# One pattern pass of the VectorE exponential moved to an accumulating GpSimd DMA

## The chip, the cores and the metric

One Trainium2 chip, one core of it. The metric is the device time of one execution, in microseconds (us), lower is better. The kernel before takes 898.37 us (median of 3 runs, 897.88 to 899.86). Experiments ran in groups on one chip each, together with new runs of the kernel before. A run counts as slow when it is over 1.5% above the fastest run of the same kernel; all are fast unless it is told otherwise.

## The reference

Two attention layers side by side, each with 2048 rows, width 512 and 32 heads of 16. A is attention within four causal segments, with a memory of the earlier segments mixed in; B is plain attention over all 2048 keys. B holds most of the exponentials, and they are what this case is about.

```python
def _B_ref(x, wqkv, wo):
    B, S, D = x.shape                     # 1, 2048, 512
    H = 32
    Dh = D // H                           # 16
    qkv = (x @ wqkv).reshape(B, S, 3, H, Dh).transpose(2, 0, 3, 1, 4)
    q, k, v = qkv[0], qkv[1], qkv[2]
    p = softmax(einsum('bhqd,bhkd->bhqk', q, k) * Dh ** -0.5)
    o = einsum('bhqk,bhkd->bhqd', p, v)
    return o.transpose(0, 2, 1, 3).reshape(B, S, D) @ wo
# _A_ref: per segment of 512 rows a causal softmax (mask) and p @ v, then
#   o = g * (phi(q) @ M) / (phi(q) @ z) + (1 - g) * a_dot;  M += phi(k)^T v;  z += sum phi(k)
# the result: concatenate([A, B], axis=-1), bf16
```

## The kernel before

The kernel is software-pipelined by its own planner. While it is built, it keeps a clock for each engine (`T["pe"]`, `T["dve"]`, `T["pool"]`, `T["sp"]` for SyncE's queue) and decides at each step what TensorE does next. What comes out is **one fixed order of instructions for each engine**; semaphores then make each wait for its inputs. If something is later on the chip than the plan assumed, TensorE does not pick other work. It waits.

Exponentials are computed in two places. ScalarE does tiles of two or three PSUM banks (`pT`). VectorE takes over whole blocks of four banks by a bit trick: it scales a score so that, as an integer, it is the bit pattern of an fp16 number near the exponential, and takes four such patterns with four offsets (`LADDER`). The products of all four with V are added in PSUM, so that their errors average out.

```python
LADDER = (12914, 13046, 13325, 13628)
VBUFS = 10                                # shared tiles of 128 x 2048 x 2 bytes
...
def v_pick():                             # start a block?
    ...
    if vlive[0] > VBUFS - 2:
        return False
    ...
            vlive[0] += 1
            x = wk.tile([P, 4, 512], U16, name="vx", tag="vx", bufs=VBUFS)
            vnow[0] = (u, kb, x, list(q4))

def v_evac(u, kb, x, j, vt, end):         # four a block: bank j of scores -> first pattern
    def f():
        pin(nc.vector.tensor_scalar(x[:, j, :], vt[:], XSCALE, float(LADDER[0]), ALU.mult, ALU.add))
        if end:
            buf = [len(LADDER)]
            v_ready(u, kb, x, buf)
            for off in LADDER[1:]:        # three pattern passes
                later(0.70, v_rung(u, kb, x, off, buf), ...)

def v_rung(u, kb, x, off, buf, pool=False):
    def f():
        vlive[0] += 1
        p = wk.tile([P, 4, 512], U16, name="vx", tag="vx", bufs=VBUFS)
        ...
        pin(nc.vector.tensor_scalar(p[:], x[:], float(off - LADDER[0]), 32767.0, ALU.add, ALU.min))
        v_ready(u, kb, p, [1], ...)
        v_done(buf)

def v_ready(u, kb, p, buf, at=None):      # from this planned time on, TensorE may read the tile
    pd = p[:].bitcast(F16)
    pvq.append(dict(u=u, kb=kb, v=buf, ready=(T["dve"] + DVEEND if at is None else at) + 0.06, ...))
```

`pin` keeps an instruction in program order against its neighbours on the engine. Two other users of SyncE's queue matter below: the eight small transfers that spread a query tile, and the transposes (four for an input chunk, four for the keys of the memory).

```python
for e in range(2):                        # do_q: eight transfers of 16 KB
    for j in range(4):
        r = slice(32 * j + DH * e, 32 * j + DH * e + DH)
        nc.sync.dma_start(out=dst[r, e, :], in_=qc[r, :])
        on_sp(0.5, T["dve"] + 0.1)
...
for cc in range(4):                       # load_xT
    nc.sync.dma_start_transpose(t[:, cc, :], xs[name][ch * W:(ch + 1) * W, cc * P:(cc + 1) * P])
```

`zero()` multiplies by zeros where TensorE would otherwise have little to do; it is meant to keep the clock up. By the planner's own count it aims at an activity of 0.52 over about 3 us, in which a product on a quarter of the array counts 0.25; that this is the right aim is not tested here.

## Time and profile before

| | before |
|---|---|
| time, median | 898.37 us |
| ScalarE busy | 866.6 of 897.7 us |
| ScalarE exponential tiles / VectorE blocks | 747 / 125 |
| VectorE busy | 796.1 us |
| TensorE waits for VectorE, all kinds | 6.7 us |
| DMA traffic | 19.85 MB, 22 GB/s |
| TensorE at half clock | 19 us |

The last row is summed from the trace's clock records (some 2 us of it, in every kernel, lie after the last instruction), and it is the one that I undervalued. From the page of the kernel before: the clock in 40 slices of 22 us, and the group of TensorE products that read VectorE's patterns (busy us, mean ns, idle us before them, what ended most of it).

```profile
PEclk9999999979999999999999999999999999999998
...
L117 PE MATMUL acc<-vx,VB 128*32 128x512 f16 x2000 | 180.8, 384 | 2.0 <-DVE vx L982 0.7
```

The clock is down in one slice only, beside the end. Stage by stage around it (us from the start; PE, PEld, DVE, ACT and POOL busy with counts; clock; DMA share; GB/s):

```profile
150.00:186.00 36.00, 30.54 (x268) 10.03 (x266) 29.60 (x55) 33.61 (x32) 11.39 (x23) 0.98 0.20 41
186.00:196.00 10.00, 9.52 (x49) 1.89 (x48) 4.90 (x9) 5.47 (x5) 2.31 (x2) 0.56 0.07 13
```

TensorE's single stop of 5 us ends at 186.5; the ten microseconds from 186 on run at a mean clock of 0.56. TensorE is busy there (9.52 of 10) and the engines that it feeds are not: ScalarE is busy for 5.47 us of 10. **The wait is paid a second time, afterwards.**

### The profile page before, as it was taken

Reading aid. Unit: us, or ns where it says so; the run is one execution under the profiler, and the core shown is the slowest. Engines: PE = TensorE matmul, PEld = TensorE weight load, DVE = VectorE, ACT = ScalarE, POOL = GpSimd, SP = SyncE. Lnnn points to the kernel's source line nnn. Section 1 sums busy time; section 2 is a strip of 40 time slices with the busy share of each in tenths; the row PEclk is TensorE's granted clock in tenths of the full one; section 3 lists DMA queues with packets and bytes.
Section 4 is the critical chain, followed back from the end, with each engine's and each line's share of the span. In section 5 each row is a group of like instructions: output and inputs, shape, how many; then the busy total and the mean of one; then the engine's idle time right before and its main releaser. Section 6 shows DMA issues by size and latency. Waiting matters only on the chain.

```text
span 897.7 us, 19235 instructions
## 1 busy us (share of the span) xinstructions
PE 863.9 (96%) x7673; PEld 258.9 (29%) x7673; DVE 796.1 (89%) x1362; ACT 866.6 (97%) x777; POOL 130.8 (15%) x295
## 2 busy tenths in 40 slices
PE   9999999979999999999999999999999999999996
PEld 3322332312323232222232322323222322222222
DVE  4786699959998998989989999999999999999994
ACT  6999999969999999999999999999999999999995
POOL 7710300310202003030110302002030300000000
PEclk9999999979999999999999999999999999999998
DMA  9600000200001201000000210000000000000000
GB/s 194 140 10 12 24 18 9 48 18 7 15 6 19 60 23 28 7 7 13 2 19 2 42 37 12 3 1 7 1 8 1 19 24 13 1 2 1 1 2 29
DMA packets 48181, 19.85 MB, mean 22 GB/s; under 512 B 37200, under 2 KB 48080, under 8 KB 48080
## 3 DMA queue, kind: packets, MB, share of 16 engines
q1 hardware_dynamic: 46736, 17.99, 9.1%
q8 instruction: 62, 1.02, 0.5%
q10 hardware_dynamic: 1344, 0.52, 0.2%
q14 instruction: 39, 0.32, 0.1%
HBM read 4.20 MB, written 4.19 MB: 9 GB/s over the span
## 4 chain that ended last, share of the span: by engine, by line
ACT 25%; PE 21%; issue 9%; DVE 5%; POOL 0%; DVEq 0%; ACTq 0%
ACT pT L893 24%; PE acc L117 11%; PE s_ps L117 6%; PE v_ps L117 2%; DVE vx L966 2%; DVE vx L982 2%; PE o_ps L117 1%; DVE tT L382 1%; ACT ex L307 0%; POOL pT L903 0%; PE l_ps L117 0%; PE q_ps L117 0%; DVE OT_b L430 0%; DVE rsum L405 0%; DVE osb L1264 0%
## 5 line engine op out<-in xcount | busy, mean ns | idle before, releaser
L893 ACT ACTIVATE pT<-s_ps 128x1536 bf16<-128x1536 f32 x747 | 854.9, 1289 | 13.0 <-PE s_ps L117 8.8
L966 DVE TENSOR_SCALAR vx<-v_ps 128x512 uint16<-128x512 f32 x500 | 328.4, 685 | 26.8 <-PE v_ps L117 21.6
L117 PE MATMUL s_ps<-qb,KB 32*128 32x512 bf16 x1548 | 249.4, 384 | 8.2 <-ACT pT L893 4.0
L982 DVE TENSOR_SCALAR vx<-vx 128x2048 uint16<-128x2048 uint16 x375 | 248.9, 693 | 5.0 <-PE v_ps L117 3.2
L117 PE MATMUL v_ps<-qb,KB 32*128 32x512 bf16 x500 | 181.8, 382 | 2.0 <-DVE vx L966 0.9
L117 PE MATMUL acc<-vx,VB 128*32 128x512 f16 x2000 | 180.8, 384 | 2.0 <-DVE vx L982 0.7
L903 POOL TENSOR_SCALAR_AFFINE_SELECT pT<-pT 128x256 bf16<-128x256 bf16 (+2 forms) x241 | 105.8, 469 | 481.8 <-ACT pT L893 481.3
L117 PE MATMUL acc<-pT,VB 128*32 128x512 bf16 x1548 | 151.6, 389 | 0.0
L117 PEld LDWEIGHTS <-KB 32*128 32x128 bf16 x2048 | 82.8, 91 | 237.1 <-issue 230.2
L117 PE MATMUL acc<-zeros 128*128 128x512 bf16 x395 | 135.4, 389 | 0.0
L117 PEld LDWEIGHTS <-VB 128*32 128x32 bf16 x3548 | 73.4, 94 | 165.6 <-issue 154.1
L117 PE MATMUL s_ps<-qa,kA 32*128 32x384 bf16 (+3 forms) x512 | 53.3, 299 | 5.3 <-ACT pT L893 3.0
L117 PEld LDWEIGHTS <-zeros 128*128 128x128 bf16 x417 | 34.2, 98 | 82.5 <-issue 77.2
L382 DVE STREAM_TRANSPOSE tT<-acc 128x512 f32<-128x512 f32 x64 | 44.9, 704 | 12.8 <-PE acc L117 12.4
L117 PE MATMUL acc<-pT,vA 128*32 128x256 bf16 (+3 forms) x512 | 33.3, 306 | 0.3 <-POOL pT L903 0.2
L117 PEld LDWEIGHTS <-kA 32*128 32x128 bf16 x512 | 17.8, 91 | 45.3 <-issue 42.3
L272 DVE CAST qc<-q_ps 128x512 bf16<-128x512 f32 x28 | 19.1, 684 | 6.8 <-PE q_ps L117 6.6
L117 PE MATMUL q_ps<-xT_a,w_a 128*128 128x512 bf16 x64 | 19.8, 386 | 5.0 <-DMA xT_a<-in_A_x_dram 5.0
L460 DVE CAST osb<-o_ps 128x512 bf16<-128x512 f32 x28 | 19.1, 683 | 4.6 <-PE o_ps L117 4.1
L416 POOL TENSOR_TENSOR tN<-tT,rsum 128x512 bf16<-128x512 f32 x1 | 1.4, 1368 | 130.1 <-DVE rsum L405 130.1
L117 PE MATMUL k_ps<-xT_a,w_a 128*128 128x512 bf16 x64 | 19.8, 398 | 0.0
L117 PE MATMUL o_ps<-wo_a,OT_a 128*128 128x512 bf16 x64 | 18.8, 383 | 0.3 <-DVE vx L966 0.2
(94 smaller groups left out, 409.7 us busy)
## 6 DMA issues: line engine op xcount, KB each, us to landing
out_dram<-osb SPq DMA_DIRECT2D x30, 128.0 KB, 1.7
w_b<-in_B_wqkv_dram SPq DMA_DIRECT2D x3, 512.0 KB, 6.0
qb<-qc SPq DMA_DIRECT2D x96, 16.0 KB, 1.8
qa<-qc SPq DMA_DIRECT2D x72, 16.0 KB, 1.8
phk<-phkT SPq DMA_TRANSPOSE x48, 2.4
w_a<-in_A_wv_dram SPq DMA_DIRECT2D x1, 512.0 KB, 5.1
wo_a<-in_A_wo_dram SPq DMA_DIRECT2D x1, 512.0 KB, 5.0
wo_b<-in_B_wo_dram SPq DMA_DIRECT2D x1, 512.0 KB, 4.9
```

Source lines behind the costliest of these rows:

```text
L117: return pin(nc.tensor.matmul(out, lhsT, rhs, **k))
L272: pin(nc.vector.tensor_copy(qc[:], ps[:]))
L382: pin(nc.vector.transpose(st["tT"][:, e].rearrange("p c d -> p (c d)"), acc[:]))
L416: pin(eng.tensor_tensor(o, tT[:, :, :, 0:DH], rr.to_broadcast(bc), op=ALU.mult))
L460: pin(nc.vector.tensor_copy(osb[:], ps[:]))
L893: pin(nc.scalar.activation(pT[:, 0:n, :], pt[:, 0:n, :], ACT.Exp, scale=SCALE))
L903: pin(nc.gpsimd.affine_select(out=blk, in_=blk, compare_op=ALU.is_ge, fill=0.0, base=0, pattern=[[0, len(sls)], [1, P]], channel_multiplie ...
L966: pin(nc.vector.tensor_scalar(x[:, j, :], vt[:], XSCALE, float(LADDER[0]), ALU.mult, ALU.add))
L982: pin(nc.vector.tensor_scalar(p[:], x[:], float(off - LADDER[0]), 32767.0, ALU.add, ALU.min))
```

## The change

The intent is to relieve VectorE of one of its three passes a block, so that it can take over more blocks from ScalarE, the bound. A tile is filled with the constant difference of the offsets by a plain DMA on SyncE's queue when the block starts. After the block's last evacuation, a DMA issued from GpSimd adds the first pattern to it (`accum_op`). Two more of the shared tiles are made, the output weights move into shared tiles, and all transfers on SyncE are pinned.

```diff
-VBUFS = 10
+VBUFS = 12
+DMARUNG = 3
+ACCPOOL = 1.05
+ACCDMA = 4.5
+FILLSP = 0.55
+FILL = 512
 ...
+        fill = wk.tile([P, 1, FILL], I16, name="fill")
+        nc.gpsimd.memset(fill[:], LADDER[DMARUNG] - LADDER[0])
 ...  v_pick
-            if vlive[0] > VBUFS - 2:
+            if vlive[0] > VBUFS - 3:
 ...
-                vnow[0] = (u, kb, x, list(q4))
+                vlive[0] += 1
+                p = wk.tile([P, 4, 512], I16, name="vx", tag="vx", bufs=VBUFS)
+                pin(nc.sync.dma_start(out=p[:].rearrange("p j (a c) -> p (j a) c", c=fill.shape[-1]),
+                                      in_=fill[:].to_broadcast([P, 2048 // fill.shape[-1], fill.shape[-1]])))
+                on_sp(FILLSP, T["pe"])
+                vnow[0] = (u, kb, (x, p), list(q4))
 ...  v_evac
-                    for off in LADDER[1:]:
-                        later(0.70, v_rung(u, kb, x, off, buf), ...)
+                    for i in range(1, len(LADDER)):
+                        if i == DMARUNG:
+                            atasks.append((T["dve"] + DVEEND, v_sum(u, kb, *x, buf)))
+                            continue
+                        later(0.70, v_rung(u, kb, x[0], LADDER[i], buf), ...)
 ...
+        def v_sum(u, kb, x, p, buf):
+            def f():
+                pin(nc.gpsimd.dma_start(out=p[:], in_=x[:], accum_op=ALU.add))
+                v_ready(u, kb, p, [1], T["pool"] + ACCDMA)
+                v_done(buf)
+            return f
 ...  pool_run
+            while atasks and (atasks[0][0] < T["pe"] + 0.1 or not live[0]):
+                ready, f = atasks.popleft()
+                on_pool(ACCPOOL, ready)
+                f()
 ...  (cut: pin() around every transfer on SyncE; output weights into shared tiles; a removed GpSimd path)
```

Note what the plan knows and does not know. It lets TensorE read the sum 1.05 + 4.5 us after the accumulation is planned to start. It lets the accumulation start when the pattern is ready, and never asks whether the fill has landed.

> **What bounds the kernel now.** I read the page's busy shares first, then the groups of ScalarE and VectorE, then the busy time stage by stage, then the one stage that stands out.
>
> The busy shares, columns: engine, busy microseconds, share of the span, instructions; below them two costly groups (busy, mean ns of one, idle before them and what ended it).
>
> ```profile
> PE 863.9 (96%) x7673; PEld 258.9 (29%) x7673; DVE 796.1 (89%) x1362; ACT 866.6 (97%) x777; POOL 130.8 (15%) x295
> ...
> L893 ACT ACTIVATE pT<-s_ps 128x1536 bf16<-128x1536 f32 x747 | 854.9, 1289 | 13.0 <-PE s_ps L117 8.8
> L966 DVE TENSOR_SCALAR vx<-v_ps 128x512 uint16<-128x512 f32 x500 | 328.4, 685 | 26.8 <-PE v_ps L117 21.6
> ...
> L982 DVE TENSOR_SCALAR vx<-vx 128x2048 uint16<-128x2048 uint16 x375 | 248.9, 693 | 5.0 <-PE v_ps L117 3.2
> ...
> L117 PE MATMUL acc<-zeros 128*128 128x512 bf16 x395 | 135.4, 389 | 0.0
> ```
>
> ScalarE does 747 exponential tiles and waits only 13.0 us ahead of them: it sets the pace. TensorE looks as full (96%), but 135.4 us of it are multiplications by zeros that only fill gaps. VectorE computes the exponentials of 125 blocks by itself: four evacuations (500 in all) and three pattern passes (375) a block. It is at 89%, with no room for many more blocks. So work leaves ScalarE only if VectorE is relieved first; that is the intent.
>
> The same by stages (us from the start; PE, PEld, DVE, ACT, POOL busy with counts; granted clock; DMA share; GB/s):
>
> ```profile
> 0.00:22.00 22.00, 20.04 (x123) 6.97 (x123) 9.08 (x18) 13.06 (x14) 16.12 (x45) 1.00 0.95 198
> 22.00:100.00 78.00, 76.55 (x626) 23.15 (x626) 58.09 (x99) 77.62 (x71) 21.70 (x53) 1.00 0.23 51
> 100.00:250.00 150.00, 141.81 (x1206) 43.08 (x1202) 128.05 (x232) 141.50 (x131) 26.77 (x55) 0.97 0.09 19
> 250.00:400.00 150.00, 146.51 (x1319) 43.56 (x1317) 138.07 (x234) 148.99 (x135) 21.16 (x47) 1.00 0.09 22
> 400.00:550.00 150.00, 146.95 (x1346) 44.06 (x1339) 141.50 (x248) 149.61 (x136) 15.37 (x33) 1.00 0.08 18
> ...
> 860.00:897.70 37.70, 29.08 (x251) 8.92 (x248) 24.90 (x46) 27.01 (x25) 0.78 (x2) 0.91 0.06 18
> ```
>
> ScalarE's 31 idle us lie at the start (22 - 13.06 = 8.9), at the end (10.7) and in one middle stage (150 - 141.5 = 8.5, granted clock 0.97); elsewhere it misses under 1 us per 150. The timeline of that middle stage shows why:
>
> ```profile
> 178.68 4.96 SPq L277 DMA_DIRECT2D qa<-qc  x8
> ...
> 183.68 1.26 SPq L234 DMA_TRANSPOSE xT_a<-in_A_x_dram  x1
> 186.48 0.59 PE L117 MATMUL q_ps<-xT_a,w_a 128*128 128x512 bf16 x1 [5.04 <-DMA xT_a<-in_A_x_dram]
> ...
> 188.63 1.45 ACT L893 ACTIVATE pT<-s_ps 128x1536 bf16<-128x1536 f32 x1 [5.02 <-PE s_ps L117]
> ```
>
> The fourth transpose of an input chunk stands in SyncE's queue behind eight small transfers of a query tile (4.96 us). TensorE, which runs its instructions in a fixed order, stands still for 5.04 us, and every engine with it.
>
> **What the Trainium skill says.** "DMA: Bandwidth & Descriptors", section "SWDGE vs HWDGE vs iDMA": accumulation during a DMA is possible only for one issued from GpSimd, which writes the descriptors in software. No accumulating transfer is in this trace, so it shows nothing of its cost. The same page, "Anatomy of one DMA", fits a transfer as 2.0 us + bytes/436 GB/s; for 512 KB that is 3.2 us (estimate from that page). Here the 512 KB weight loads from HBM land 4.9 to 6.0 us after issue, so it is optimistic for those. "SBUF — State Buffer", section "Who interferes with whom": a VectorE instruction in a two-port mode and GpSimd lock each other out, and descriptor writing suffers. The trace fits: GpSimd's 128x128 mask of 0.352 us mean took 0.80 us where it began together with a pattern pass, at 444.60 us:
>
> ```profile
> 444.60 0.65 DVE L982 TENSOR_SCALAR vx<-vx 128x2048 uint16<-128x2048 uint16 x1
> 444.60 0.80 POOL L903 TENSOR_SCALAR_AFFINE_SELECT pT<-pT 128x128 bf16<-128x128 bf16 x1 [44.84 <-ACT pT L893]
> ```
>
> **The change, part by part.** Counts come from the order of the built instructions, durations from the rows above.
>
> ScalarE: VectorE blocks go from 125 to 132, so ScalarE loses 7 blocks of four banks: 1868 banks become 1840. A bank costs 854.9/1868 = 0.458 us, so 28 banks are 12.8 us. This is on the path.
>
> VectorE: evacuations 500 to 528, +28 x 0.657 (328.4/500) = +18.4 us; pattern passes 375 to 264, -111 x 0.664 = -73.7 us. Busy falls from 796 to about 741 us. Worth nothing directly; the seven blocks are what it buys. The plan takes so few although VectorE is freed: a block now holds two of the 12 tiles from its first score on, and none may start above nine live.
>
> TensorE: 112 more products with the pattern tiles (+10.1 us at 180.8/2000), 28 more single scores (+10.2), 28 fewer tile scores and products (-7.2), 23 fewer zero products (-7.9): +5 us, inside what zeros fill today.
>
> DMA: 132 fills and 132 accumulations of 512 KB, 138 MB beside today's 19.85 MB: some 156 GB/s on average over 885 us. It fits the engines, but each accumulation also reads its destination; if that doubles the moved part of the fit, it needs 2.0 + 2 x 1.2 = 4.4 us (estimate). The diff plans with 1.05 us on GpSimd and 4.5 us to land.
>
> GpSimd: 132 issues at about 1.05 us, +139 us, to about 270 of 885: not a bound, but in order with the causal masks.
>
> SyncE's queue: the diff pins every transfer to program order. In the new order the four transposes of the chunk of 174.8 us stand together, and the query tile follows. The hole at 183 us should go: -8.5 us, on the path. I count this as surely as the ScalarE term.
>
> What is given back. TensorE's order is fixed, so a late pattern tile stops it. By ScalarE's pace (0.458 us a bank) I counted, in the built order, from the last score of a block to the first reader of its accumulated tile: median 7.8 us, tenth percentile 6.9, shortest 3.2. Score and evacuation take 0.38 + 0.69 us plus signalling, some 1.4; 5.5 are left at the tenth percentile, against 1.05 + 4.4 = 5.5. It just fits. The chain that starts at the fill is tighter: 3.2 + 1.05 + 4.4 = 8.7 us, against a median of 10.5 from the fill's place in SyncE's queue to the reader. About 14 fills stand over 2 us behind query tiles (4.93 us for eight transfers) and transposes (some 5 us for four). Nine blocks have under 8.7 us: 1.9, 5.5, 5.5, 5.9, 6.0, 7.4, 7.7, 7.8, 8.5; shortfalls sum to 22 us. ScalarE has about one tile, 1 us, in hand each time, which leaves 13; a few will overlap other slack. I take +9 us.
>
> Sum: 898.4 - 12.8 - 8.5 + 9 = 886 us.
>
> **Rivals.** First, the accumulation is slower than planned, or GpSimd's descriptors are held up by the two remaining passes, which start just when the accumulation is issued (both follow the last evacuation). 107 of the 132 tiles are read as the last of their block, some at the planned moment; 1 us more than the slack on a hundred blocks gives about +80 us after what ScalarE has in hand: 960. For it: the 0.80 us mask above, and no measurement of this kind of transfer. Against it: the diff's constants look like measured ones, and leave that slack. Second, everything lands in time: 898.4 - 21.3 = 877 us, 2.4% faster. For it: ScalarE's other waits are tiny. Against it: the nine blocks. Third, transfers of fills and accumulations lengthen each other and the query tiles (now 1.8 us to landing), a few us per chunk: 895 to 905. Fourth, VectorE's relief is worth more than the seven blocks: hardly, as ScalarE waits so little elsewhere.
>
> **Range and chances.** The sure terms sum to -21 us, and 2% is 18 us; 3.4 us of new waits suffice to fall under it. I give 0.23 to faster, 0.57 to within 2%, and 0.20 to slower, nearly all of it the first rival. Range 870 to 915.
>
> **What would show it.** ScalarE's tiles at 736 and busy near 854 us; VectorE near 741; no 5 us wait for the A input near 180 us and a clock of 1.00 there; waits of TensorE's products for an accumulating DMA, in a handful of places of 2 to 6 us, behind SyncE's query tiles; issue to landing of the accumulations near 4 to 5.5 us, of the fills near 3 to 4. Wrong: waits for that DMA at most blocks (first rival), or almost none (second); ScalarE's idle time in the middle over 20 us without any DMA behind it would mean that I have missed a mechanism.

## The result, and the profile after

The changed kernel took 972.3 us (median of 4 runs, 966.53 to 975.56), the kernel before 899.09 us on the same occasion (897.88 to 899.86). The ratio is 1.0809 (95% interval 1.075 to 1.0867): 8% slower, and outside the predicted range. Ratios here are the mean time of one kernel's fast runs over that of the other's of the same rounds, so not quite the ratio of the medians quoted.

From the page after: busy shares; groups; clock; issues with their median time to landing.

```profile
PE 885.0 (91%) x7730; PEld 257.3 (27%) x7730; DVE 754.4 (78%) x1280; ACT 860.9 (89%) x766; POOL 245.3 (25%) x431
...
PEclk9999998989969989799798997999999999899999
...
L910 ACT ACTIVATE pT<-s_ps 128x1536 bf16<-128x1536 f32 x736 | 848.7, 1274 | 88.6 <-PE v_ps L121 48.5
L988 DVE TENSOR_SCALAR vx<-v_ps 128x512 uint16<-128x512 f32 x528 | 348.9, 686 | 114.0 <-PE v_ps L121 106.3
L1002 POOL DMA_DIRECT2D vx<-vx x132 | 121.9, 924 | 606.4 <-DVE vx L988 476.1
...
L121 PE MATMUL acc<-vx,VB 128*32 128x512 f16 x2112 | 199.5, 402 | 53.7 <-DMA vx<-vx 52.0
...
L1011 DVE TENSOR_SCALAR vx<-vx 128x2048 uint16<-128x2048 uint16 x264 | 179.8, 690 | 3.6 <-DMA vx<-vx 2.0
...
vx<-fill SPq DMA_DIRECT2D x132, 512.0 KB, 4.7
vx<-vx POOLq DMA_DIRECT2D x132, 512.0 KB, 5.2
```

The work moved as planned: ScalarE has 736 tiles, VectorE 264 passes. No engine is the bound by its work any more. ScalarE's wait ahead of its tiles rose from 13.0 to 88.6 us, and the clock is down in ten slices (two before). The products that read VectorE's patterns, which had waited 2.0 us, wait 53.7, of which 52.0 for the accumulating transfer. Its median of 5.2 us to landing is about what the plan has (1.05 + 4.5 = 5.55); asked for all 132, the trace gives a minimum of 4.5, a median of 5.2 and a maximum of 8.1 us. The fills give 3.2, 4.7 and 8.5.

The view of waits after (us in total, times, longest):

```profile
PE acc L121 <- DMA vx<-vx: 52.0, 31, 10.5
ACT pT L910 <- PE v_ps L121: 48.5, 44, 10.3
...
POOL vx L1002 <- DMA vx<-fill: 40.7, 5, 17.8
```

Only 31 waits, not one for each of 132 blocks, and the longest is 10.5 us. The timeline shows how that one came about. First SyncE's queue (start, us, engine, line, what, times):

```profile
254.18 5.61 SPq L281 DMA_DIRECT2D qa<-qc  x8
260.21 4.96 SPq L342 DMA_TRANSPOSE phk<-phkT  x4
265.29 3.97 SPq L959 DMA_DIRECT2D vx<-fill  x4
```

then GpSimd, TensorE and ScalarE (in brackets the idle time before, and what ended it):

```profile
271.13 0.86 POOL L1002 DMA_DIRECT2D vx<-vx  x1 [17.76 <-DMA vx<-fill]
...
277.27 0.62 PE L121 MATMUL acc<-vx,VB 128*32 128x512 f16 x4 [10.48 <-DMA vx<-vx]
...
278.53 1.02 ACT L910 ACTIVATE pT<-s_ps 128x1024 bf16<-128x1024 f32 x1 [10.26 <-PE v_ps L121]
```

Four fills stand behind eight query transfers and four transposes in one queue. The fill lands just before 271.13, the accumulation needs 6.1 us more, and the products that the fixed order put there stop TensorE, and with it everything, for 10.5 us. Its stages:

```profile
250.00:268.00 18.00, 16.19 (x142) 4.76 (x135) 16.03 (x28) 18.00 (x18) 0.88 (x1) 1.00 0.35 84
268.00:286.00 18.00, 8.73 (x56) 1.83 (x55) 4.57 (x7) 4.77 (x5) 2.58 (x3) 0.53 0.81 203
286.00:300.00 14.00, 13.48 (x137) 4.16 (x135) 12.69 (x23) 13.69 (x13) 2.91 (x3) 1.00 0.83 208
```

The clock fell to half at 268.7 us and stayed there for 17.1 us, well past the end of the wait: ScalarE was busy for 4.77 of 18 us. In the stage after, the clock is full and ScalarE is busy for 13.69 of 14 us, with as much traffic (208 GB/s), so traffic of that size does not by itself stop it.

**The half clock.** The Trainium skill, "TensorE: Matmul & The Clock Gate", section "Part 1: The HAM clock gate (the "warmup" mystery)", says that TensorE's clock is full or half, decided by how busy it was in windows of about 3.4 us, and its section "HAM oscillation — how this bites in real kernels" tells of a kernel that waits for DMA and starts each tile at half clock. The traces agree: the records know only 1.0 and 0.5, and the half periods away from the ends, in these two traces, last 3.4, 6.8, 10.2, 13.7 or 17.1 us. They sum to 111 us after and 19 us before. I could have read this before predicting, from the stage of 0.56 above, and did not.

A much shorter stop can be enough. This one is from the same kernel, a wait of 0.93 us that began at 321.2 us and had nothing to do with an accumulation:

```profile
322.15 0.37 PE L121 MATMUL v_ps<-qb,KB 32*128 32x512 bf16 x1 [0.93 <-DVE osb L466]
```

and the stages before and after 323.3 us:

```profile
319.50:323.30 3.80, 2.87 (x27) 0.74 (x26) 2.91 (x6) 3.12 (x4) 0.00 (x0) 1.00 0.78 235
323.30:326.70 3.40, 3.40 (x13) 0.68 (x13) 2.31 (x4) 2.73 (x4) 0.84 (x1) 0.50 0.70 237
```

Over all seventeen traces of this case (before, after and the fifteen experiments; TensorE's stops that began at full clock, from 25 us on), this is how often a half period began by 3.5 us after the stop:

| length of the stop, us | stops | followed by half clock |
|---|---|---|
| 0.8 to 1 | 39 | 7 |
| 1 to 1.5 | 44 | 12 |
| 1.5 to 2 | 31 | 24 |
| 2 to 3 | 41 | 35 |
| over 3 | 45 | 45 |

So a wait is not worth its length alone: in these traces a stop of over 2 us was followed by a half period in 80 of 86 cases, one of 0.5 to 0.8 us in 16 of 97. (Some short stops have other stops close by. Of those with none over 0.5 us within 3.5 us, 3 of 29 of 0.8 to 1 us and 11 of 40 of 1 to 1.5 us were followed by one.)

**Where the 71 us went.** The spans differ by 968.7 - 897.7 = 71.0 us. ScalarE's busy time fell by 5.7 (866.6 to 860.9), so its idle time rose by 76.7. Directly, TensorE's waits for accumulations are 52. The half clock grew by 92 us; the rest, about 25 us, is 0.27 of that. The 0.27 is an estimate fitted to this one trace, not a measured cost; the experiments below test it.

**Behind the 52 us.** Followed block by block (130 of the 132 could be matched), 45 accumulated tiles were read within 0.3 us of landing, so TensorE stood ready for them, or nearly. For 21 blocks the fill landed after the last evacuation. 14 of the 45 stand behind such late fills, and TensorE's waits for these sum to 37 of the 52 us; all those fills came after query tiles or transposes in SyncE's queue. The other 15 us stand behind fills that were in time; there the accumulation took longer than the plan had room for (of all 132, 53 needed more than the planned 5.55 us, and about a tenth over 6.8).

### The profile page after: what moved, and what is told of

Same layout as the page of the kernel before. It is cut to its first block, busy times and chain, and to the rows that moved or that the text cites. A ratio compares the mean times of both kernels' runs of the same rounds, so it can differ in the third digit from the quotient of the medians.

```text
span 968.7 us, 19889 instructions
## 1 busy us (share of the span) xinstructions
PE 885.0 (91%) x7730; PEld 257.3 (27%) x7730; DVE 754.4 (78%) x1280; ACT 860.9 (89%) x766; POOL 245.3 (25%) x431
## 3 DMA queue, kind: packets, MB, share of 16 engines
q1 hardware_dynamic: 116176, 87.07, 29.6%
## 4 chain that ended last, share of the span: by engine, by line
PE 32%; DMA 22%; issue 21%; ACT 13%; DVE 8%; POOL 2%; SPq 1%; POOLq 0%; DVEq 0%; ACTq 0%
DMA vx<-vx 15%; PE acc L121 14%; ACT pT L910 12%; PE s_ps L121 9%; DMA vx<-fill 5%; PE v_ps L121 5%; DVE vx L988 3%; POOL vx L1002 2%; PE o_ps L121 2%; DVE vx L1011 2%; PE k_ps L121 1%; PE q_ps L121 1%; ACT ex L311 1%; SPq L238 1%; DVE tT L386 1%
## 5 line engine op out<-in xcount | busy, mean ns | idle before, releaser
L910 ACT ACTIVATE pT<-s_ps 128x1536 bf16<-128x1536 f32 x736 | 848.7, 1274 | 88.6 <-PE v_ps L121 48.5
L988 DVE TENSOR_SCALAR vx<-v_ps 128x512 uint16<-128x512 f32 x528 | 348.9, 686 | 114.0 <-PE v_ps L121 106.3
L1002 POOL DMA_DIRECT2D vx<-vx x132 | 121.9, 924 | 606.4 <-DVE vx L988 476.1
L121 PE MATMUL s_ps<-qb,KB 32*128 32x512 bf16 x1520 | 259.2, 400 | 8.5 <-ACT pT L910 6.0
L121 PE MATMUL acc<-vx,VB 128*32 128x512 f16 x2112 | 199.5, 402 | 53.7 <-DMA vx<-vx 52.0
L121 PE MATMUL v_ps<-qb,KB 32*128 32x512 bf16 x528 | 196.7, 402 | 3.5 <-DVE vx L988 1.5
L1011 DVE TENSOR_SCALAR vx<-vx 128x2048 uint16<-128x2048 uint16 x264 | 179.8, 690 | 3.6 <-DMA vx<-vx 2.0
L121 PE MATMUL acc<-pT,VB 128*32 128x512 bf16 x1520 | 155.4, 405 | 0.0
L121 PEld LDWEIGHTS <-VB 128*32 128x32 bf16 x3632 | 79.3, 95 | 232.3 <-issue 219.6
L121 PE MATMUL k_ps<-xT_b,w_b 128*128 128x512 bf16 x64 | 20.0, 399 | 0.2 <-DVE tT L386 0.2
```

The lines of the kernel that those rows point to most:

```text
L121: return pin(nc.tensor.matmul(out, lhsT, rhs, **k))
L910: pin(nc.scalar.activation(pT[:, 0:n, :], pt[:, 0:n, :], ACT.Exp, scale=SCALE))
L988: pin(nc.vector.tensor_scalar(x[0][:, j, :], vt[:], XSCALE, float(LADDER[0]), ALU.mult, ALU.add))
L1002: pin(nc.gpsimd.dma_start(out=p[:], in_=x[:], accum_op=ALU.add))
```

## The experiments

The first explanation was: *the pattern tiles come late against the fixed order, because the plan leaves too little time for accumulation, or fill, or both.* Rivals: SyncE's queue alone; the traffic itself (163 GB/s) slows everything; the rest of the change (pins, twelve buffers, output weights) does it; GpSimd's descriptor writing is locked out by VectorE. The expectations name theories as they stood at that time; where one missed, it is said below.

Fifteen kernels ran, in four groups on different occasions; all were correct. Medians of the kernel before in the groups: 897.69 (first four kernels below: pins, fill by GpSimd DMA, memset, fill in the plan), 897.27 (7.0, 3.0, all late, no DMA pass), 898.18 (6.0, 8.5, 7.0 with hold, 7.0 with fill and query), 897.91 (the last three). Two other builds did not run. One, meant to add the traffic without the dependence, did not fit into SBUF, so **traffic alone was never tried**. The other (7.0 with the fill landing in the plan) was REFUSED by the check: an accumulation was left unissued at the end of the plan, and an uninitialised read followed; it was mended as the run "7.0 with fill and query".

### Pins alone

```diff
 kernel before
-            nc.sync.dma_start_transpose(t[:, cc, :], ...)
+            pin(nc.sync.dma_start_transpose(t[:, cc, :], ...))
 ... the same on every other SyncE transfer
```

> The kernel before, with nothing changed but that every SyncE transfer is pinned to program order; the order on TensorE is identical, 125 blocks and 747 ScalarE tiles. If the 5.04 us wait for the A input (and the 10.2 us of half clock after it) is priced as I priced it in the prediction, -8.5 us: about 890 us. Rival: the pin moves a transfer that delays something else, or the hole costs nothing in the end: 897 to 900.

Measured: 898.44 us, ratio 1.0013 [0.9991, 1.0035]; TensorE's order is unchanged. Timeline around the middle hole of this run:

```profile
175.12 4.94 SPq L277 DMA_DIRECT2D qa<-qc  x8
180.16 5.11 SPq L234 DMA_TRANSPOSE xT_a<-in_A_x_dram  x4
...
186.77 1.02 ACT L893 ACTIVATE pT<-s_ps 128x1024 bf16<-128x1024 f32 x1 [4.59 <-PE s_ps L117]
```

The first reading, 890 us, missed; its rival, 897 to 900, came true. The pins are free, and useless by themselves. The transposes now stand together, behind the query transfers instead of around them, and the hole stays.

### The rest of the change without the DMA pass

```diff
 changed kernel
-DMARUNG = 3
+DMARUNG = 99                             # all three passes on VectorE
-            if vlive[0] > VBUFS - 3:
+            if vlive[0] > VBUFS - 2:
-                p = wk.tile(...); fill by DMA; on_sp(...)
+                p = None
 ... (shortened; the small tile's constant is kept)
```

> Everything else of the change kept (12 shared tiles with the output weights in them, pinned transfers), but all three passes on VectorE again and no fill, no accumulation; 125 blocks, 747 tiles. Both theories: 895 to 902, as the loss is in the DMA pass. If it is above 920, the reshuffled buffers or pins carry part of the loss.

Measured: 900.98 us, 1.004 [1.0018, 1.0063], 125 blocks and 747 tiles as before. Twelve buffers, moved output weights and pins cost at most 0.6%. The loss is in the DMA pass.

### The fill from GpSimd's queue, or by GpSimd itself

```diff
 changed kernel, first run
-                pin(nc.sync.dma_start(out=p[:]..., in_=fill[:]...)); on_sp(FILLSP, T["pe"])
+                pin(nc.gpsimd.dma_start(out=p[:]..., in_=fill[:]...)); on_pool(0.95, T["pe"])
 second run
+                pin(nc.gpsimd.memset(p[:], LADDER[DMARUNG] - LADDER[0])); on_pool(1.95, T["pe"])
```

> The changed kernel with the fills issued from GpSimd instead of SyncE: the same DMA traffic, but no fill stands behind query tiles and transposes. Theory 1 (fills late in SyncE's queue cause most of the loss, by waits and the half clock that follows them): waits of TensorE for accumulations fall from 52 us to about 15, the mean granted clock rises from 0.943 to above 0.97, time about 915. Theory 2 (the accumulations themselves land too late, or the DMA traffic slows everything): waits stay near 50 us and the time stays above 955. Plan: 128 blocks, 743 tiles.

> The changed kernel with each fill done by a GpSimd memset instead of a DMA: half the added DMA traffic, and nothing of it in SyncE's queue. 120 blocks and 755 ScalarE tiles in its plan, so +3.7 us of ScalarE work against before. Theory 1: no late fills, accumulations land in 4.5 to 5 us; waits under 10 us, time about 900. Theory 2 with the accumulation itself as the cause: waits stay over 40 us, time above 950; theory 2 with traffic as the cause: faster than the run with the fills issued from GpSimd by 20 us or more.

Measured: fill by a DMA from GpSimd 972.4 us, 1.0817 [1.0782, 1.0853]. TensorE still waits 41 us for accumulations; the fills need 6.1 us instead of 4.7. Both theories named were off: waits are nearer to 50 than to 15 us, and the time is that of the second. SyncE's queue is not the only way to be late; the fill is as late from another (GpSimd waits 44 us for fills here, 41 us in the changed kernel).

Fill by GpSimd memset: 962.04 us, 1.0712 [1.0685, 1.0738], with the traffic halved to 82.9 MB. TensorE's waits for accumulations are nearly gone (3.1 us), as theory 1 had it; its time of about 900 us missed. In their place, from its waits:

```profile
PE acc L121 <- DVE vx L1010: 23.3, 35, 3.4
```

TensorE now waits for VectorE, in all 41.6 us against 6.7 before. The passes and the memsets, from the groups of the page of this run (busy us, mean ns):

```profile
L959 POOL MEMSET vx<- 128x2048 int16 x120 | 240.8, 2064 | 17.2 <-PE acc L121 13.3
L1010 DVE TENSOR_SCALAR vx<-vx 128x2048 uint16<-128x2048 uint16 x240 | 213.4, 905 | 1.2 <-PE acc L121 0.7
```

A pass takes 905 ns in the mean here (median 683, longest 3137) and 690 in the changed kernel (median 684, longest 1339): some passes stand for a whole memset. That is the lock that the prediction feared, but it shows where GpSimd computes, not where it issues transfers: of the 75 passes over 1 us in all seventeen traces, 74 lie beside a computing instruction of GpSimd, such as a memset or a mask. An issue took 0.86 us (median) in the changed kernel; the 71 that ran beside a pass took 0.97 us in the mean, the other 61 took 0.87. The memset trades one wait for another, and half the traffic does not help as long as TensorE is made to wait.

### The fill's landing in the plan

```diff
 changed kernel
+FLAND = 4.2
+                fat[id(p)] = T["sp"] + FLAND
-                            atasks.append((T["dve"] + DVEEND, v_sum(...)))
+                            atasks.append((max(T["dve"] + DVEEND, fat[id(x[1])]), v_sum(...)))
```

> The changed kernel, but the plan counts an accumulation as issuable only once the fill has landed by its own account of SyncE's queue (issue plus 4.2 us); the transfers are the same, only TensorE's and the other orders move. 134 blocks, 733 ScalarE tiles. Theory 1: the late fills are planned for, so the waits fall to about 15 to 20 us and the time to 905 to 920. Theory 2: as the accumulation's planned time is untouched, waits stay near 50 us and the time above 955.

Measured: 952.96 us, 1.0615 [1.0577, 1.0653], 134 blocks, 733 tiles. The waits for accumulations fall from 52 to 29.6 us, but VectorE now waits 19.5 us for them (probably since tiles come free later), and the half clock is 100 us. An improvement of 2%, between the two theories; the known late fills are part of the cause, not all of it.

### The planned time to landing, as a dose

```diff
 changed kernel
-ACCDMA = 4.5
+ACCDMA = 3.0        # and 6.0, 6.5, 7.0, 7.5, 8.5 in other runs
```

> The opposite dose: 3.0 us instead of 4.5; 133 blocks; from the last score to the reader 6.0 us in the median. Theory 1: most of the 133 tiles are waited for, some 1.5 us each over what now is; waits over 130 us, time above 1030. Theory 2: about 970, as the traffic is the same.

> Third point of the dose: an accumulation planned to land 6.0 us after issue; 130 blocks, 739 tiles as with 7.0. The plan then allows 1.05 + 6.0 = 7.05 us from the issue, which about nine landings in ten kept (6.8 us in the changed kernel). Theory 1: few waits are left, under 25 us on accumulations, time 905 to 920, between 898 and 972. If it is at 898 or below, 7.0 was more than needed; above 940 would mean that the step from 4.5 to 7.0 is not about lateness but about that one order.

> 6.5 us, between 6.0 (904.7) and 7.0 (898.0); 130 blocks and 739 tiles in all three. If the time follows the planned landing: 896 to 906. If it follows chance in the order of the transfers (any change of order draws anew): anywhere from 895 to 950.

> The changed kernel with one constant of its plan moved: an accumulation is planned to land 7.0 us after GpSimd's issue instead of 4.5; 130 blocks, 739 ScalarE tiles; from the last score to the reader of the accumulated tile 8.2 us at least and 10.5 in the median (7.8 before). Theory 1, as it now stands (accumulated tiles land later than the fixed order of TensorE supposes; each wait also halves the clock for some us): waits on accumulations under 15 us, half-clock time under 60 us, time 915 to 930. Theory 2 (the transfers slow the engines or other transfers, whenever they are read): above 955.

> 7.5 us, between 7.0 (898.0) and 8.5 (935.7); 130 blocks, 739 tiles. If a longer planned landing by itself brings the second loss back: 905 to 925, and waits of VectorE on accumulations between 9 and 37 us. If the loss at 8.5 is chance of the order: 895 to 905 is as likely.

> Fourth point: 8.5 us; 131 blocks, 738 tiles. Theory 1: there is little left to win by it, waits on accumulations near 0, time 888 to 902; if tiles are held too long it starts to cost in blocks, but its plan has as many. No reading of theory 2 makes it faster than with 7.0.

| planned, us | blocks / tiles | median, us | ratio [95%] | TensorE waits for accumulations | VectorE waits for them | half clock |
|---|---|---|---|---|---|---|
| 3.0 | 133 / 735 | 1041.7 | 1.1624 [1.1583, 1.1664] | 92.5 | 3.9 | 159 |
| 4.5 (the change) | 132 / 736 | 972.3 | 1.0809 [1.075, 1.0867] | 52.4 | 3.7 | 111 |
| 6.0 | 130 / 739 | 904.67 | 1.0062 [1.0039, 1.0086] | 17.3 | 10.7 | 37 |
| 6.5 | 130 / 739 | 909.93 | 1.0147 [1.0127, 1.0167] | 13.8 | 2.6 | 33 |
| 7.0 | 130 / 739 | 897.96 | 1.0024 [0.9984, 1.0064] | 7.1 | 9.1 | 19 |
| 7.5 | 130 / 739 | 912.34 | 1.0183 [1.0146, 1.022] | 16.1 | 7.4 | 36 |
| 8.5 | 131 / 738 | 935.71 | 1.0411 [1.0392, 1.043] | 3.8 | 37.0 | 68 |

(The waits of this table are summed per instruction from the traces, all in us; the page counts those of 4.5 as 52.0. With 3.0, two of six runs were slow ones, and they are in the median. The other four took 1027.6 to 1042.7 us, mean 1036.2, which is 1.154 times the kernel before; the recorded ratio of 1.1624 is not the mean of these four, but the verdict is the same.) The pages of 3.0 and 7.0, the clock, and for 7.0 the busy shares and the products that read patterns:

```profile
PEclk9999989989989888899998999997899998979898
```

```profile
PE 843.5 (94%) x7640; PEld 256.6 (29%) x7698; DVE 742.2 (83%) x1268; ACT 858.2 (96%) x769; POOL 241.2 (27%) x428
...
PEclk9999999999999999999899999999999999999998
...
L121 PE MATMUL acc<-vx,VB 128*32 128x512 f16 x2080 | 187.1, 387 | 13.1 <-DMA vx<-vx 7.0
```

One constant of the planner, changed by 2.5 us, takes back all of the loss: 972 to 898. It moves no work to speak of (132 to 130 blocks) and leaves the transfers as they were, 156 MB at 174 GB/s. **That settles the main question: lateness against the fixed order is the cause; the traffic costs next to nothing where, as with 7.0, the plan leaves time for it.** The opposite dose, 3.0, makes it worse as expected of lateness, though with 62 waits and 92.5 us of them, not "most of the 133" and over 130. With 6.0, 6.5 and 7.5 the plan takes back 60 to 68 of the 74 us; that 7.0 takes back all of it, more than its expectation of 915 to 930, may be luck of the order.

The number of accumulations that landed later than planned falls with the dose: 133 of 133 with 3.0, 53 of 132 with 4.5, then 22, 10, 9, 4 and 1 of some 130. 7.0 + 1.05 = 8.05 us is about the longest landing that the changed kernel's trace had (8.1), 4.5 + 1.05 somewhat above the median; in the run with 7.0 itself the longest was 9.6.

The traffic does have a part in it: it makes the landings spread. In the changed kernel, accumulations with at most one other 512 KB transfer under way in their first microsecond landed after 4.8 us in the median (69 of them), with two after 5.6 (49), with three or more after 7.0 (14). In the memset run, with half the traffic, the longest was 6.1.

Past 6.0 the doses do not line up: 905, 910, 898, 912, 936; the expectation for 8.5, 888 to 902, missed. 6.5 lies above its 896 to 906 and 7.5 within its 905 to 925, but with fewer waits of VectorE than expected. With 8.5 TensorE hardly waits for accumulations, but VectorE does, 33.5 of its 37 us at its passes:

```profile
DVE vx L1011 <- DMA vx<-vx: 33.5, 16, 6.1
...
PE acc L121 <- DMA vx<-vx: 3.8, 3, 2.4
```

A pass needs a free shared tile, and gets one that an accumulation still reads or writes. I took this for the plan's early release (`v_done` right after the issue) and tried to mend it.

### Released at landing; all landings late

```diff
 changed kernel with ACCDMA = 7.0, and with 8.5
-                v_done(buf)
+                frees.append((T["pool"] + ACCDMA, buf))
+            while frees and (frees[0][0] < T["pe"] or not live[0]):
+                v_done(frees.popleft()[1])
 "7.0 with fill and query": ACCDMA = 7.0, no hold; FLAND = 4.2 as above, and
-                        on_sp(0.5, T["dve"] + 0.1)
+                        on_sp(0.62, T["dve"] + 0.1)
 "all late": ACCDMA = 7.0 with hold, FLAND = 5.5, on_sp(0.75, ...)
```

> The version with 7.0 us, plus one of the three further corrections of the run that had all: the block's first tile is held in the plan until the accumulation that reads it has landed; 131 blocks, 738 tiles. That run was 917 where 898 was expected. If the held tile is its cause: 910 to 920. If not: 893 to 902, as VectorE's waits on an accumulation (8.9 us with 7.0) go away.

> 8.5 us, and the block's first tile held in the plan until the accumulation that reads it has landed; 129 blocks, 741 tiles. At 8.5 without the hold, TensorE no longer waited for accumulations (3.8 us), but VectorE did, for tiles still in use by one (37 us, 19 times). If that early release is the second loss, the hold takes VectorE's waits under 10 us and the time to 895 to 910. If it stays above 925, with VectorE's waits small, the fills late in SyncE's queue (GpSimd waits 73 us for them) are the cause; with VectorE's waits as large, the tile waited for is another one.

> The version with 7.0 us, plus the other two corrections in their measured size: the fill lands 4.2 us after its place in the queue, a query-tile transfer takes 0.62 us of SyncE (4.96/8); 131 blocks, 738 ScalarE tiles, 9 fewer than before. If it meets no new wait, ScalarE's 9 tiles are worth 10 us: 885 to 892, faster than the kernel before by about 1%. If the shift of other work brings waits back, as in the run with all corrections: 905 to 920.

> The plan told the truth throughout: fill landing 5.5 us after its place in SyncE's queue, query-tile transfers 0.75 us each, landing 7.0 us after issue, and the block's first tile held until the accumulation that reads it has landed; 128 blocks, 743 tiles. Theory 1: waits on accumulations under 5 us, half-clock time as in the kernel before (10 to 20 us), time 895 to 905, so no slower than before by more than 1%. Theory 2: still above 940.

| run | blocks / tiles | median, us | ratio [95%] | TensorE waits for accumulations | VectorE waits for them | half clock |
|---|---|---|---|---|---|---|
| 7.0, released at landing | 131 / 738 | 948.59 | 1.0587 [1.052, 1.0655] | 25.2 | 17.3 | 96 |
| 8.5, released at landing | 129 / 741 | 911.91 | 1.0174 [1.0138, 1.021] | 6.7 | 11.4 | 34 |
| 7.0 with fill and query | 131 / 738 | 923.94 | 1.0297 [1.0275, 1.0319] | 5.2 | 27.2 | 47 |
| all late | 128 / 743 | 917.4 | 1.0216 [1.0183, 1.0248] | 0 | 17.6 | 43 |

Releasing at landing took 24 us off at 8.5 (VectorE's waits fell from 37.0 to 11.4) and put 51 us on at 7.0. Neither time lies in a range that was expected. The early release is therefore not shown to be the cause, and I leave it. "7.0 with fill and query" missed both of its ranges too. The all-late plan removes TensorE's waits for accumulations altogether and is still 2% slower than before (expected: 895 to 905 us and 10 to 20 us of half clock): VectorE waits 17.6 us for tiles that accumulations hold, TensorE 23.7 us for VectorE, and the half clock is twice that of before. A plan that counts more truths is not a faster one here; each changes the whole order, and with it, I suppose without having checked it, the places where fills happen to stand behind a query tile.

**How far the bookkeeping carries.** The sum "TensorE's waits for accumulations, plus its waits for VectorE above the 6.7 us of before, plus 0.27 of the half clock above the 19 us of before" against the measured rise of ScalarE's idle time, in us, for the runs to which the factor was not fitted:

| run | sum | ScalarE's idle time, added |
|---|---|---|
| 3.0 | 138 | 129 |
| 6.0, 6.5, 7.0, 7.5 | 23, 20, 12, 22 | 16, 16, 6, 19 |
| 8.5 | 39 | 43 |
| released at landing: 7.0, 8.5 | 48, 16 | 56, 17 |
| 7.0 with fill and query; all late | 31; 24 | 30; 24 |
| fill by GpSimd DMA; by memset; in the plan | 68; 50; 66 | 73; 49; 65 |

It is off by up to 9 us and sorts the runs rightly but for neighbours. So the spread past 6.0 is a spread of TensorE's stops and of the half periods that follow them. Why a given order has them where it has them stays open.

No version beat the kernel before. The best, 7.0, equals it.

## Why the prediction was wrong

1. **ScalarE's relief, -12.8 us: half right.** 747 tiles became 736 as counted. Busy time fell by 5.7 us, not 12.8; the row of the tiles itself fell by 6.2 (854.9 to 848.7). In the run with 7.0, where little disturbs, 8 fewer tiles (20 banks, 9.2 us by the prediction's rate) gave 8.4 us, so the size of the term was about right for an undisturbed kernel. The changed kernel's tiles did not cost more: one of three banks took 1486 ns against 1500, one of two 1063 against 1078 (means). But tiles that follow each other at once overlap in the records, by 108 us in all before and by 89 after, and busy time counts an overlap once; a tile after a wait overlaps nothing.
2. **VectorE near 741 us: 754.4**, from 528 evacuations and 264 passes as counted; nothing hung on it.
3. **The pins, -8.5 us: mostly wrong.** The pins alone gave 1.0013, and the middle hole stayed in that run. In the changed kernel the four transposes of A's input stand together ahead of the query tile as predicted, but behind another query tile and eight other transposes, from 171.8 to 187.8 us without a break; TensorE waited for them four times (3.5 us), the clock dropped for 6.8 us, and ScalarE was idle for 5.3 us of the 30 from 170 to 200. I had looked at the order of two neighbours in the queue and not at what stood ahead of both.
4. **The time to landing: right in the middle, wrong as a use.** Accumulations were expected near 4 to 5.5 us; the median was 5.2, the longest 8.1. Fills were estimated at 3 to 4; the median was 4.7, the longest 8.5. (The fit that gave their 3.2 is the page's for transfers issued from GpSimd, and the fills are issued from SyncE.)
5. **The step that failed is "What is given back": "It just fits", and "I take +9 us".** I compared the tenth percentile of the slack with one figure for the landing, and took the agreement for no cost. Both sides spread: 45 of 130 tiles were read within 0.3 us of landing, and the waits sum to 52 us instead of the 13 left of my 22. I had listed nine tight blocks and 14 fills behind query tiles and transposes; 21 fills came too late, and the waits behind them alone sum to 37 us. My subtraction of "about one tile, 1 us, in hand each time" also failed: waits of up to 10.5 us came in 31 places, not in a few.
6. **The term that I left out altogether is the clock.** TensorE's stops dropped it to half for 92 us more than before; by my estimate that is some 25 us of the 71. The one such stage in the trace before, at 0.56, lay under the lines that I quoted, and I counted its hole, not its tail.
7. **The first rival (960 us) came nearest, for half the right reason.** Its size, "1 us more than the slack on a hundred blocks", was wrong: 31 waits. Its lock of GpSimd by VectorE does not show: 0.86 us an issue, passes unchanged at 690 ns. Its "no measurement of this kind of transfer" was the part to heed: I trusted the diff's 4.5 us because it looked measured, and it is a median where a high percentile is needed. The third rival, transfers lengthening each other, is right as a mechanism (accumulations of 4.8 us in the median with little beside them, 7.0 with three or more transfers; output transfers with 3.1 against 1.7 us to landing). Its size, 895 to 905, was not: the lengthening costs by what TensorE's order does not allow for, and with 7.0 the same traffic cost nothing.

## What to carry to other kernels

In a kernel with a fixed order of instructions, plan an asynchronous transfer near its longest landing and not at its median, and measure that landing beside the traffic that it will meet; here 2.5 us more in one constant was worth 74 us, and moved hardly any work. Then measure around the value: 1.5 us more again lost 38 us. Judge waits by their longest ones: in these traces 80 of 86 stops of TensorE over 2 us were followed by a period of half clock. When work leaves an engine for a DMA, list what already stands in that queue, and count the chain from its start (fill, then accumulation), not its last link.

## What the Trainium skill lacked or had wrong

- "TensorE: Matmul & The Clock Gate", in its Part 1, ties the half clock to an idle window of about 3.4 us and gives no count for shorter stops. In this kernel, with most products on a quarter of the array, far shorter stops sufficed at times: 7 of 39 stops of 0.8 to 1 us, 24 of 31 of 1.5 to 2 us, all 45 over 3 us. The half periods came in steps of 3.4 us, the length of the page's window, up to 20.5 us.
- "DMA: Bandwidth & Descriptors" says who may issue an accumulating transfer, but no duration. 512 KB within SBUF, added in int16: 4.5 us shortest, 5.2 median, 8.1 longest from issue to landing, in a kernel that moves 163 GB/s; 4.5 to 6.1 in the memset run at 86 GB/s. The issue takes GpSimd 0.83 to 1.35 us (median 0.86).
- The same page's fit, made for transfers that GpSimd issues, gives 3.2 us for 512 KB. The plain fills within SBUF took 3.3 us at best, 6.1 in the median and 9.1 at worst when GpSimd issued them, and 3.2, 4.7 and 8.5 from SyncE, each time beside other transfers: the fit is the best case here, and a plan needs the tail, which no page gives.
- "SBUF — State Buffer" says that VectorE's two-port modes and GpSimd lock each other out and that descriptor writing suffers. The first part shows in the memset run (passes of 905 ns mean, 3137 longest). The second hardly does: an issue 0.86 us (median), at most 1.35, and passes at 690 ns against 693 before. The case of that page's section "A bandwidth-pool intuition that's wrong (but worth ruling out)", a transfer of about 620 ns that takes about 3100 beside a VectorE copy, has no match here.
